# The first product of each expert in two halves of 512 columns, and the low terms of the second product last in each half

## The chip, the cores and the metric

The kernel runs on one core of a Trainium2 chip. A core has a matrix engine (TensorE, PE in the profile; its weight loads stand in a row of their own, PEld), VectorE (DVE), ScalarE (ACT), GpSimd (POOL) and SyncE (SP), which here issues most transfers. The engines run their own instructions in order and wait for each other by semaphores. The metric is the time of one execution in microseconds on the device.

## The reference

Attention with a window of 32 positions and 32 global tokens per batch gives 1088 rows of 512 numbers. A gate sends each row to the expert with the highest logit, up to 288 rows an expert, and a dense network of two products follows. The middle part is the one that matters here (sizes by the inputs: E = 8 experts, D = 512, F = 1024, capacity 288):

```python
logits = x @ w_gate
expert_idx = np.argmax(logits, axis=1)
...
disp[e, counts[e]] = x[i]          # if counts[e] < capacity
...
h = np.maximum(np.einsum('ecd,edf->ecf', disp, w1), 0.0)
y = np.einsum('ecf,efd->ecd', h, w2)
...
out[i] = gate_w[i] * y[expert_idx[i], pos[i]]
```

## The kernel before

The kernel is one program in three stages: attention with the gate, the experts, and the dense network. The order of instructions on each engine is the order in which the Python code writes them; no scheduler moves them, and the semaphores follow from the tiles that are read and written.

Products are made in float32r, each operand as a high part (rounded) and a low part (what the rounding left). A product is three terms: high times high, high times low, and low times high. So each weight chunk that lands (`raw`, 128x1024) is rounded to `H` by `weight_h` (L218 on ScalarE, L220 on VectorE for one chunk in eight) and the rest taken to `L` by `weight_l` (L230 on VectorE). Each expert has eight such chunks, four of w1 and four of w2, and its successor's chunks are converted while it runs. `split` (L598, L599) does the same for the rows: ScalarE rounds from PSUM, VectorE subtracts.

An expert's rows come in groups of 128, 128 and 32. The first group always runs (the first tile). The second and the third stand under branches on the expert's count (`rest`, the branch tiles). `expert_tile` makes one group. `mm1(q)` multiplies the rows with 256 columns of w1 in one PSUM buffer (8 matmuls with the high rows, 4 with the low rows) and takes the relu on ScalarE into `hs`. `tr(q)` turns `hs` by two transposes into a PSUM buffer of tag T, which has two, and splits that into `hh` and `hl`. `mm2(k)` multiplies the k-th 128 of them with 128 rows of w2: high with H, high with L, low with H, all eight into one PSUM buffer `py`. `bg()` is called eight times in a first tile and writes the background work: the weight conversions, the copy of the last expert's `py` to `ys` (L810), small steps for the gates, in experts 6 and 7 steps of the next stage's weights (L248 to L285), and in the third call the load of the expert's count into registers with a hint for the branch (L889 to L891). `mid(0)` turns the next expert's rows (`x_prep`, tiles `mx`, `x0h`, `x0l`). After expert 7 the rows of two token tiles are multiplied into the next stage's input, of which VectorE makes the low part at L1139.

Of the kernel before, what the change touches and what calls it, by code (L numbers as in the profile page):

```python
# [8 lines left out]
F32 = mybir.dt.float32  # L9
# [4 lines left out]
AF = mybir.ActivationFunctionType  # L14
# [4 lines left out]
P = 128  # L19
# [9 lines left out]
def tile_attention_moe_ffn(  # L29
# [23 lines left out]
    nc = tc.nc  # L53
# [10 lines left out]
    KD = DM // P  # L64
    KF = F // P
# [21 lines left out]
    def ps_tile(tag, name, hold=False):  # L87

        bank = psum[tag].pop(0)
        (held.setdefault(name, []) if hold else psum[tag]).append(bank)  # L90
        return pspool.tile([P, 512], F32, tag=bank, name=name, bufs=2 if bank == "T" else 1)
# [5 lines left out]
    def ps_a(name):  # L97
        return ps_tile("A", name)

    def ps_t(name):  # L100
        return ps_tile("T", name)
# [173 lines left out]
    def wide_h(g, c):  # L275
        if c == 0:
            unit_tiles(2 * E + g, 8)
        H, L = HL[2 * E + g]
        sl = slice(c * 512, (c + 1) * 512)
        nc.scalar.copy(H[:, sl], CV[g, c])  # L280

    def wide_l(g, c):
        H, L = HL[2 * E + g]
        sl = slice(c * 512, (c + 1) * 512)
        nc.vector.tensor_tensor(out=L[:, sl], in0=CV.pop((g, c)), in1=H[:, sl].bitcast(F32), op=ALU.subtract)  # L285
# [311 lines left out]
    def split(dst_h, dst_l, src):  # L597
        nc.scalar.copy(dst_h, src)  # L598
        nc.vector.tensor_tensor(out=dst_l, in0=src, in1=dst_h.bitcast(F32), op=ALU.subtract)  # L599
# [13 lines left out]
    for i in range(2):  # L613
        t = at.tile([P, 576], F32, name=f"pg{i}")
# [64 lines left out]
    for k in range(NS):  # L679
# [14 lines left out]
        if 5 <= k < 13:  # L694
            c = k - 5
# [38 lines left out]
    for ns, k0 in ((range(5), range(KD)),):  # L734
        for n in ns:
            x, at_ = parts[n]
# [24 lines left out]
    mo = mctx.enter_context(tc.tile_pool(name="mo", bufs=1))  # L761
# [50 lines left out]
    def base_store(e, eng):  # L812
        rows = groups[0][1]
        eng.dma_start(yd[1 + e * cap:1 + e * cap + rows, :], YB[e][:rows])
# [8 lines left out]
    def expert_tile(e, j, bg, mid):  # L823

        nm = f"{e}_{j}"
        rows = groups[j][1]
        w1h, w1l = W[2 * e]
        w2h, w2l = W[2 * e + 1]
        xh, xl = XH.pop((e, j))
        HS = {}  # L830
        hh = mo.tile([P, F], F32R, tag="hh", name=f"hh{nm}", bufs=1).rearrange("p (k t) -> p k t", k=KF)
        hl = mo.tile([P, F], F32R, tag="hl", name=f"hl{nm}", bufs=1).rearrange("p (k t) -> p k t", k=KF)
        py = ps_tile("V" if j and e < E - 1 else "Y", f"py{nm}")

        def mm1(q):
            ph = ps_a(f"ph{nm}{q}")
            fs = slice(256 * q, 256 * q + 256)
            for k in range(KD):
                nc.tensor.matmul(ph[:rows, :256], xh[:, k, :rows], w1h[:, k, fs], start=k == 0, stop=False)  # L839
                nc.tensor.matmul(ph[:rows, :256], xh[:, k, :rows], w1l[:, k, fs], start=False, stop=False)  # L840
            for k in range(KD):
                nc.tensor.matmul(ph[:rows, :256], xl[:, k, :rows], w1h[:, k, fs], start=False, stop=k == KD - 1)  # L842
            HS[q] = mo.tile([P, 256], F32, tag="hs", name=f"hs{nm}{q}", bufs=3)
            nc.scalar.activation(HS[q][:rows], ph[:rows, :256], AF.Relu)  # L844

        def tr(q):
            pt = ps_t(f"pt{nm}{q}")
            hs = HS.pop(q)
            for k in range(2):
                nc.tensor.transpose(pt[:, k * P:k * P + rows], hs[:rows, k * P:(k + 1) * P], ident[:rows, :rows])  # L850
            split(hh[:, 2 * q:2 * q + 2, :rows], hl[:, 2 * q:2 * q + 2, :rows],
                  pt[:, :256].rearrange("p (k t) -> p k t", k=2)[:, :, :rows])

        def mm2(k):
            a, c = hh[:, k, :rows], hl[:, k, :rows]
            nc.tensor.matmul(py[:rows], a, w2h[:, k, :], start=k == 0, stop=False)  # L856
            nc.tensor.matmul(py[:rows], a, w2l[:, k, :], start=False, stop=False)  # L857
            nc.tensor.matmul(py[:rows], c, w2h[:, k, :], start=False, stop=k == KF - 1)  # L858

        bg()  # L860
        mm1(0)
        mm1(1)
        bg()
        tr(0)
        mm1(2)
        bg()
        tr(1)
        mm1(3)
        bg()
        tr(2)  # L870
        mm2(0)
        mid(0)
        bg()
        mm2(1)
        tr(3)
        mm2(2)
        mid(1)
        bg()
        mm2(3)
        mm2(4)  # L880
        bg()
        mm2(5)
        mm2(6)
        bg()
        mm2(7)
        return py

    def count(e):
        vals[e] = nc.values_load(cnt[0:1, e:e + 1], engines=engs, min_val=0, max_val=cap)  # L889

        tc.mark_branch_hint_location(f"rest{e}_1", (vals[e] + (P - 1)) >> 8, engines=(ENG.PE, ENG.DVE, ENG.Activation))  # L891
# [96 lines left out]
    def job_h(u, c):  # L988
        weight_h(u, c, nc.vector if 4 * (u % 2) + c == 3 else nc.scalar)

    def job_l(u, c):
        weight_l(u, c, nc.vector)
        if wn[0] < len(wl) + 6:
            next_w()
# [8 lines left out]
    hl = [[lambda c=c: wide_h(0, c), lambda c=c: wide_l(0, c)] for c in range(4)]  # L1003
# [8 lines left out]
    for e in range(E):  # L1012
# [3 lines left out]
        def bg():  # L1016
            n = nbg[0]
            nbg[0] += 1
            if e > 0 and n == 2:
                count(e)  # L1020
            while late_l:
                job_l(*late_l.pop(0))
            for job in todo[:((2, 1, 1, 1, 1, 1, 1, 0) if e < E - 3 else (2, 2, 1, 1, 1, 1, 0, 0))[n]]:
                del todo[:1]
                job_h(*job)

                late_l.append(job)
            for f in wide[n] if wide else ():
                f()
            if e > 0 and small:  # L1030
                small.pop(0)()
            if n == (e < E - 1) and py_last is not None:
                base_out(*py_last)
                if e == E - 1:
                    base_store(e - 1, nc.sync)
            if n == 2 and py_last is not None and e < E - 1:
                base_store(e - 1, nc.sync)
            if e == 0 and n == 7:
                for i in range(E):
                    for r0, rows in groups[1:]:  # L1040
                        nc.sync.dma_start(yd[1 + i * cap + r0:1 + i * cap + r0 + rows, :], zero[:rows])
            if e == E - 1:
                for f in own.get(n, ()):
                    f()

        def mid(i):
            if i == 1 and e == 0:
                count(e)
            if i == 0 and e + 1 < E:
                x_prep(e + 1, 0)  # L1050
                if e + 2 < E:
                    x_load(e + 2, 0, 1)

        rest_load(e)
        py = expert_tile(e, 0, bg, mid)
# [78 lines left out]
    for h in range(2):  # L1134
        px = OWN["x"][h].rearrange("p (k n) -> p k n", k=2)
        xh, xl = (x.rearrange("p (a h) n -> p h a n", h=2)[:, h] for x in XC[0])
# [83 lines left out]
    ph = []  # L1220
# [189 lines left out]
```

## Time and profile before

| | us |
|---|---|
| median of 3 runs | 478.09 |
| lowest and highest | 477.2, 481.27 |
| the profiled execution | 479.32 |
| its span, first to last instruction | 477.5 |

| engine | busy us | share of the span |
|---|---|---|
| PE | 451.1 | 94% |
| PEld | 395.5 | 83% |
| DVE | 337.6 | 71% |
| ACT | 245.3 | 51% |
| POOL | 96.4 | 20% |

The rows further down come from one profiled execution. In a timeline a row is a start, a duration and an instruction or several alike; a matmul's duration includes its pipeline, so the distance between starts tells what one costs in a stream. In brackets stands how long the engine was idle before and what ended that; "issue" names nothing that the profile shows.

### The profile page before, as it was taken

What the parts mean: (1) busy time and instruction counts of PE and PEld (TensorE: products, weight loads), DVE (VectorE), ACT (ScalarE), POOL (GpSimd) and SP (SyncE); (2) the same over time, 40 slices, a digit from 0 to 9 for tenths busy, and PEclk for the clock granted to TensorE, in tenths of its full rate; (3) what the DMA queues carried; (4) which work ended last, traced back from release to release, by engine and by line L of the source; (5) the groups of instructions that cost most, each with busy time, mean ns of one, the idle gap of its engine ahead of it and who ended that gap; (6) DMA issues with size and microseconds to landing.
All of it is one profiled execution on the core that took longest, in us unless ns stands there. A gap on an engine that the chain in (4) does not pass through costs nothing. (4 is left out here: it accounts for less than half of the span.)

```text
span 477.5 us, 8782 instructions
## 1 busy us (share of the span) xinstructions
PE 451.1 (94%) x3163; PEld 395.5 (83%) x3164; DVE 337.6 (71%) x739; ACT 245.3 (51%) x556; POOL 96.4 (20%) x98
## 2 busy tenths in 40 slices
PE   8998899999999989899989799998999999999997
PEld 4776677788787878788878699998999999999997
DVE  4787498683166397754987875777788888979633
ACT  4768566273253466644776476455444344343311
POOL 1114355300000000000001271322213222232221
PEclk9999799999999998999999799999999999999999
DMA  8999544579348189982895531363222220000103
GB/s 267 289 329 364 184 143 134 184 271 366 138 145 286 56 275 298 333 286 75 275 347 176 168 113 56 113 231 113 75 89 89 88 89 1 1 0 1 66 1 121
DMA packets 34600, 79.24 MB, mean 166 GB/s; under 512 B 3761, under 2 KB 8497, under 8 KB 34546
## 3 DMA queue, kind: packets, MB, share of 16 engines
q1 hardware_dynamic: 31698, 70.40, 44.2%
q0 software_dynamic: 1408, 4.46, 2.9%
q10 hardware_dynamic: 1440, 3.67, 2.3%
q8 instruction: 33, 0.54, 0.5%
q14 instruction: 21, 0.17, 0.1%
HBM read 63.77 MB, written 14.75 MB: 164 GB/s over the span
## 5 line engine op out<-in xcount | busy, mean ns | idle before, releaser
L1157 PE MATMUL fh<-oldH,H 128*128 128x256 f32 (+1 forms) x256 | 66.8, 338 | 4.6 <-DVE oldH L1139 2.9
L230 DVE TENSOR_TENSOR L<-raw,H 128x1024 fp32r<-128x1024 f32 x56 | 66.8, 1218 | 1.8 <-issue 1.0
L218 ACT CAST H<-raw 128x1024 fp32r<-128x1024 f32 x57 | 59.3, 1061 | 15.2 <-PEq L896 13.0
L1197 PE MATMUL acc<-oldH,H 128*128 128x256 f32 (+2 forms) x240 | 65.0, 332 | 1.4 <-ACT H L280 1.0
L1157 PEld LDWEIGHTS fh<-oldH,H 128*128 128x128 f32 x256 | 46.9, 199 | 7.7 <-DVE oldH L1139 3.2
L1171 DVE SCALAR_TENSOR_TENSOR r<-r 128x256 f32<-128x256 f32 (+2 forms) x48 | 31.3, 652 | 23.6 <-ACT r L1162 23.5
L599 DVE TENSOR_TENSOR hl<-pt,hh 128x256 fp32r<-128x256 f32 (+1 forms) x48 | 19.3, 403 | 39.6 <-ACT hh L598 38.6
L1197 PE MATMUL acc<-oldH,L 128*128 128x256 f32 (+2 forms) x144 | 47.2, 328 | 0.0
L1197 PEld LDWEIGHTS acc<-oldH,H 128*128 128x128 f32 x240 | 43.3, 189 | 4.2 <-ACT H L280 1.5
L1183 ACT CAST oldH<-g 128x256 fp32r<-128x256 f32 (+2 forms) x36 | 17.9, 496 | 55.5 <-DVE g L1175 55.5
L844 ACT ACTIVATE hs<-ph 128x256 f32<-128x256 f32 (+1 forms) x48 | 18.6, 388 | 47.6 <-PE ph L842 46.6
L1157 PE MATMUL fh<-oldH,L 128*128 128x448 f32 (+1 forms) x128 | 42.5, 333 | 0.0
L1184 POOL TENSOR_TENSOR oldH<-g,oldH 128x256 fp32r<-128x256 f32 (+2 forms) x24 | 26.9, 1120 | 76.9 <-ACT oldH L1183 59.3
L856 PE MATMUL py<-H,hh 128*128 128x512 f32 (+1 forms) x96 | 40.6, 423 | 0.0
L1162 ACT ACTIVATE r<-fh,half 128x256 f32<-128x256 f32 (+2 forms) x48 | 27.1, 564 | 23.2 <-PE fh L1157 22.7
L839 PE MATMUL ph<-H,x0h 128*128 128x256 f32 x128 | 34.5, 301 | 4.0 <-PEq L896 2.1
L858 PE MATMUL py<-H,hl 128*128 128x512 f32 (+1 forms) x96 | 38.1, 397 | 0.0
L857 PE MATMUL py<-L,hh 128*128 128x512 f32 (+1 forms) x96 | 37.6, 392 | 0.0
L285 DVE TENSOR_TENSOR L<-co,H 128x512 fp32r<-128x512 f32 x32 | 23.2, 731 | 19.0 <-ACT H L280 19.0
L1157 PE MATMUL fh<-oldL,H 128*128 128x384 f32 x128 | 35.3, 340 | 0.4 <-DVE g L1175 0.4
L932 POOL DMA_INDIRECT yg_own<-yd,idx x2 | 2.3, 1138 | 156.7 <-ACT hs L844 156.4
L324 ACT ACTIVATE sm<-sm,ng 128x224 f32<-128x224 f32 x64 | 30.1, 477 | 4.6 <-DVE ng L313 4.5
(202 smaller groups left out, 1102.1 us busy)
## 6 DMA issues: line engine op xcount, KB each, us to landing
raw<-in_w_dram SPq DMA_DIRECT2D x64, 512.0 KB, 5.8
raw<-in_w_in_dram SPq DMA_DIRECT2D x14, 512.0 KB, 5.1
raw<-in_w_out_dram SPq DMA_DIRECT2D x12, 512.0 KB, 3.7
xd<-zero SPq DMA_DIRECT2D x16, 256.0 KB, 6.0
vt<-in_vx_dram SPq DMA_DIRECT2D x8, 320.0 KB, 5.0
xt<-xd SPq DMA_DIRECT2D x8, 256.0 KB, 5.0
yd<-zero SPq DMA_DIRECT2D x8, 256.0 KB, 4.6
yd<-ys SPq DMA_DIRECT2D x8, 256.0 KB, 4.8
```

Source lines behind the costliest of these rows:

```text
L218: nc.scalar.copy(dst, src)
L230: eng.tensor_tensor(out=L[:, sl], in0=RAW.pop((u, c)), in1=H[:, sl].bitcast(F32), op=ALU.subtract)
L324: nc.scalar.activation(SM[s][:, c, :], SM[s][:, c, :], AF.Exp, bias=NG[s][:, c:c + 1], scale=-1.0, accum_out=SUM[b][:, i, col:col + 1])
L839: nc.tensor.matmul(ph[:rows, :256], xh[:, k, :rows], w1h[:, k, fs], start=k == 0, stop=False)
L856: nc.tensor.matmul(py[:rows], a, w2h[:, k, :], start=k == 0, stop=False)
L857: nc.tensor.matmul(py[:rows], a, w2l[:, k, :], start=False, stop=False)
L858: nc.tensor.matmul(py[:rows], c, w2h[:, k, :], start=False, stop=k == KF - 1)
L1157: nc.tensor.matmul(ph[:, :n], w[:, k, :], XC[c][i // 2][:, k, :], start=n_ == 0, stop=n_ == len(terms) - 1)
L1162: nc.scalar.activation(RS[f % 2][:, :n], ph[:, :n], AF.Relu, bias=half, scale=0.5)
L1171: nc.vector.scalar_tensor_tensor(out=r[:, :n], in0=r[:, :n], scalar=1.0, in1=r[:, :n], op0=ALU.min, op1=ALU.mult)
L1184: nc.gpsimd.tensor_tensor(out=gl[:, :n], in0=gt[:, :n], in1=gh[:, :n].bitcast(F32), op=ALU.subtract)
L1197: nc.tensor.matmul(a[:, :n], p[:, ds], q, start=f == 0 and i == 0, stop=f == nfl - 1 and i == 2)
```

## The change

The first product is made in two halves of 512 columns instead of four quarters of 256, with 24 matmuls instead of 48. A half can be written in parts: the second half's first four matmuls stand ahead of the first half's transposes. The relu and both steps of the split work on 512 columns, twice a tile instead of four times. `hs` has one buffer of 512 columns instead of three of 256. In the second product each half of four k takes its eight matmuls with high rows first and its four with low rows last. The calls of `bg` and `mid` stand at other places of the tile, in the same number.

```diff
--- before.py
+++ after.py
@@ -827,62 +827,61 @@
         w1h, w1l = W[2 * e]
         w2h, w2l = W[2 * e + 1]
         xh, xl = XH.pop((e, j))
-        HS = {}
+        HS, HP = {}, {}
         hh = mo.tile([P, F], F32R, tag="hh", name=f"hh{nm}", bufs=1).rearrange("p (k t) -> p k t", k=KF)
         hl = mo.tile([P, F], F32R, tag="hl", name=f"hl{nm}", bufs=1).rearrange("p (k t) -> p k t", k=KF)
         py = ps_tile("V" if j and e < E - 1 else "Y", f"py{nm}")
 
-        def mm1(q):
-            ph = ps_a(f"ph{nm}{q}")
-            fs = slice(256 * q, 256 * q + 256)
-            for k in range(KD):
-                nc.tensor.matmul(ph[:rows, :256], xh[:, k, :rows], w1h[:, k, fs], start=k == 0, stop=False)
-                nc.tensor.matmul(ph[:rows, :256], xh[:, k, :rows], w1l[:, k, fs], start=False, stop=False)
-            for k in range(KD):
-                nc.tensor.matmul(ph[:rows, :256], xl[:, k, :rows], w1h[:, k, fs], start=False, stop=k == KD - 1)
-            HS[q] = mo.tile([P, 256], F32, tag="hs", name=f"hs{nm}{q}", bufs=3)
-            nc.scalar.activation(HS[q][:rows], ph[:rows, :256], AF.Relu)
+        def mm1(q, lo, hi):
+            if lo == 0:
+                HP[q] = ps_a(f"ph{nm}{q}")
+            fs = slice(512 * q, 512 * q + 512)
+            terms = [(xh, w, k) for k in range(KD) for w in (w1h, w1l)] + [(xl, w1h, k) for k in range(KD)]
+            for i in range(lo, hi):
+                x, w, k = terms[i]
+                nc.tensor.matmul(HP[q][:rows], x[:, k, :rows], w[:, k, fs], start=i == 0, stop=i == len(terms) - 1)
+            if hi == len(terms):
+                HS[q] = mo.tile([P, 512], F32, tag="hs", name=f"hs{nm}{q}", bufs=1)
+                nc.scalar.activation(HS[q][:rows], HP.pop(q)[:rows], AF.Relu)
 
         def tr(q):
             pt = ps_t(f"pt{nm}{q}")
             hs = HS.pop(q)
-            for k in range(2):
+            for k in range(4):
                 nc.tensor.transpose(pt[:, k * P:k * P + rows], hs[:rows, k * P:(k + 1) * P], ident[:rows, :rows])
-            split(hh[:, 2 * q:2 * q + 2, :rows], hl[:, 2 * q:2 * q + 2, :rows],
-                  pt[:, :256].rearrange("p (k t) -> p k t", k=2)[:, :, :rows])
-
-        def mm2(k):
-            a, c = hh[:, k, :rows], hl[:, k, :rows]
-            nc.tensor.matmul(py[:rows], a, w2h[:, k, :], start=k == 0, stop=False)
-            nc.tensor.matmul(py[:rows], a, w2l[:, k, :], start=False, stop=False)
-            nc.tensor.matmul(py[:rows], c, w2h[:, k, :], start=False, stop=k == KF - 1)
+            split(hh[:, 4 * q:4 * q + 4, :rows], hl[:, 4 * q:4 * q + 4, :rows],
+                  pt.rearrange("p (k t) -> p k t", k=4)[:, :, :rows])
+
+        def mm2(q, lo, hi):
+
+            terms = [(hh, w, k) for k in range(4) for w in (w2h, w2l)] + [(hl, w2h, k) for k in range(4)]
+            for i in range(lo, hi):
+                h, w, k = terms[i]
+                nc.tensor.matmul(py[:rows], h[:, 4 * q + k, :rows], w[:, 4 * q + k, :],
+                                 start=q == i == 0, stop=q == 1 and i == len(terms) - 1)
 
         bg()
-        mm1(0)
-        mm1(1)
+        mm1(0, 0, 12)
         bg()
+        mm1(1, 0, 4)
         tr(0)
-        mm1(2)
         bg()
+        mm1(1, 4, 12)
+        bg()
+        mm2(0, 0, 6)
         tr(1)
-        mm1(3)
-        bg()
-        tr(2)
-        mm2(0)
+        mm2(0, 6, 9)
         mid(0)
         bg()
-        mm2(1)
-        tr(3)
-        mm2(2)
+        mm2(0, 9, 12)
+        mm2(1, 0, 1)
         mid(1)
         bg()
-        mm2(3)
-        mm2(4)
+        mm2(1, 1, 6)
         bg()
-        mm2(5)
-        mm2(6)
+        mm2(1, 6, 10)
         bg()
-        mm2(7)
+        mm2(1, 10, 12)
         return py
 
     def count(e):
```

ScalarE, first tile of expert 2, as it stands before (`raw` casts are the background work, `ys` the last product's copy):

```order
L218 CAST H_2379<-raw_1_1970 128x1024
L820 UNCONDITIONAL_BRANCH
L844 ACTIVATE hs_00_2397<-ph_00_2384 128x256
L844 ACTIVATE hs_01_2412<-ph_01_2399 128x256
L218 CAST H_2379<-raw_2_2025 128x1024
L810 COPY ys_2422<-py_0_1930 128x512
L598 CAST hh_0_2376<-pt_00_2424 128x256
L844 ACTIVATE hs_02_2442<-ph_02_2429 128x256
L889 TENSOR_LOAD cnt
L891 ISA
L1406 BRANCH_PREFETCH_HINT
L598 CAST hh_0_2376<-pt_01_2478 128x256
```

and as it stands with the change:

```order
L218 CAST H_2163<-raw_1_1847 128x1024
L820 UNCONDITIONAL_BRANCH
L845 ACTIVATE hs_00_2181<-ph_00_2168 128x512
L218 CAST H_2163<-raw_2_1894 128x1024
L810 COPY ys_2191<-py_0_1822 128x512
L598 CAST hh_0_2160<-pt_00_2198 128x512
L888 TENSOR_LOAD cnt
L890 ISA
L1405 BRANCH_PREFETCH_HINT
L845 ACTIVATE hs_01_2247<-ph_01_2193 128x512
L218 CAST H_2252<-raw_0_1942 128x1024
L598 CAST hh_0_2160<-pt_01_2262 128x512
```

The second relu stands behind the first copy to `hh` and the count's load instead of ahead of the third cast, and two entries of 512 columns stand for four of 256.

TensorE, the same tile, around its first transposes, before:

```order
L840 MATMUL ph_01_2399<-L_1932,x0h 128x256
L842 MATMUL ph_01_2399<-H_1931,x0l 128x256 x4
L850 MATMUL pt_00_2424<-ident,hs_00_2397 128x128 x2
L839 MATMUL ph_02_2429<-H_1931,x0h 128x256
L840 MATMUL ph_02_2429<-L_1932,x0h 128x256
L839 MATMUL ph_02_2429<-H_1931,x0h 128x256
```

and with the change:

```order
L842 MATMUL ph_00_2168<-H_1823,x0l 128x512 x4
L842 MATMUL ph_01_2193<-H_1823,x0h 128x512
L842 MATMUL ph_01_2193<-L_1824,x0h 128x512
L842 MATMUL ph_01_2193<-H_1823,x0h 128x512
L842 MATMUL ph_01_2193<-L_1824,x0h 128x512
L851 MATMUL pt_00_2198<-ident,hs_00_2181 128x128 x4
L888 TENSOR_LOAD cnt
L890 ISA
L1405 BRANCH_PREFETCH_HINT
L842 MATMUL ph_01_2193<-H_1823,x0h 128x512
L842 MATMUL ph_01_2193<-L_1824,x0h 128x512
```

The transposes of `hs` have four matmuls between them and the last one of their own half, where they had twelve, and the count's load follows them.

TensorE, the same tile, where the second product begins, before:

```order
L850 MATMUL pt_02_2505<-ident,hs_02_2442 128x128 x2
L856 MATMUL py_0_2378<-H_2053,hh_0_2376 128x512
L857 MATMUL py_0_2378<-L_2054,hh_0_2376 128x512
L858 MATMUL py_0_2378<-H_2053,hl_0_2377 128x512
L798 MATMUL mx_0_0_2513<-ident,xt_0_2072 128x128 x4
L856 MATMUL py_0_2378<-H_2053,hh_0_2376 128x512
L857 MATMUL py_0_2378<-L_2054,hh_0_2376 128x512
L858 MATMUL py_0_2378<-H_2053,hl_0_2377 128x512
L850 MATMUL pt_03_2530<-ident,hs_03_2496 128x128 x2
```

and with the change:

```order
L860 MATMUL py_0_2162<-L_1913,hh_0_2160 128x512
L851 MATMUL pt_01_2262<-ident,hs_01_2247 128x128 x4
L860 MATMUL py_0_2162<-H_1912,hh_0_2160 128x512
L860 MATMUL py_0_2162<-L_1913,hh_0_2160 128x512
L860 MATMUL py_0_2162<-H_1912,hl_0_2161 128x512
L798 MATMUL mx_0_0_2272<-ident,xt_0_1939 128x128 x4
L860 MATMUL py_0_2162<-H_1912,hl_0_2161 128x512 x3
L860 MATMUL py_0_2162<-H_1912,hh_0_2160 128x512
```

The matmuls with `hl` stand ninth to twelfth of a half instead of each third, and the second transposes behind six matmuls with `hh`.

## Rows read from the trace of the kernel before

**Rows 1.** The page's part 1: busy time, share of the span and instructions.

```profile
PE 451.1 (94%) x3163; PEld 395.5 (83%) x3164; DVE 337.6 (71%) x739; ACT 245.3 (51%) x556; POOL 96.4 (20%) x98
```

**Rows 2.** Windows, first tiles of experts 3, 4, 6: length, busy us, clock, DMA.

```profile
175.10:191.60 16.50, 14.32 (x84) 12.85 (x85) 13.35 (x22) 10.44 (x19) 0.00 (x0) 0.90 0.92 301
191.60:206.70 15.10, 13.51 (x88) 11.73 (x88) 12.22 (x21) 10.47 (x19) 0.00 (x0) 1.00 0.97 328
234.60:249.20 14.60, 13.04 (x85) 11.20 (x85) 12.98 (x16) 11.73 (x20) 0.00 (x0) 1.00 0.99 357
```

**Rows 3.** Groups by line: busy us, mean ns | idle before, releasers.

```profile
L599 DVE TENSOR_TENSOR hl<-pt,hh 128x256 fp32r<-128x256 f32 (+1 forms) x48 | 19.3, 403 | 39.6 <-ACT hh L598 38.6 <-ACTq L896 1.0
...
L844 ACT ACTIVATE hs<-ph 128x256 f32<-128x256 f32 (+1 forms) x48 | 18.6, 388 | 47.6 <-PE ph L842 46.6 <-DVE L L230 0.6
...
L599 DVE TENSOR_TENSOR x0l<-mx,x0h 128x512 fp32r<-128x512 f32 x7 | 4.8, 683 | 0.1
...
L810 ACT COPY ys<-py 128x512 f32<-128x512 f32 (+1 forms) x9 | 4.7, 540 | 1.4 <-PE py L858 1.4
...
L598 ACT CAST x0h<-mx 128x512 fp32r<-128x512 f32 x7 | 4.3, 612 | 0.0
```

**Rows 4.** Timeline of VectorE, experts 6 and 7: start, us, what, [idle before].

```profile
239.92 0.42 DVE L599 TENSOR_TENSOR hl<-pt,hh 128x256 fp32r<-128x256 f32 x1 [1.23 <-ACT hh L598]
...
269.84 1.29 DVE L1139 TENSOR_TENSOR oldH<-po,oldH 128x512 fp32r<-128x512 f32 x2 [2.01 <-DVEq L896]
```

**Rows 5.** Waits of PE: total us, times, longest.

```profile
PE fh L1157 <- DVE oldH L1139: 2.9, 1, 2.9
...
PE ph L842 <- DVE xl L599: 1.4, 2, 0.8
...
PE pt L850 <- DVE hl L599: 0.6, 2, 0.3
```

**Rows 6.** Timeline of PE, expert 0, first tile.

```profile
98.10 0.28 PE L839 MATMUL ph<-H,x0h 128*128 128x256 f32 x1
...
98.69 0.28 PE L840 MATMUL ph<-L,x0h 128*128 128x256 f32 x1
...
103.88 0.39 PE L856 MATMUL py<-H,hh 128*128 128x512 f32 x1
...
106.61 0.39 PE L856 MATMUL py<-H,hh 128*128 128x512 f32 x1
```

**Rows 7.** Timeline of ACT, expert 2.

```profile
161.62 2.00 ACT L218 CAST H<-raw 128x1024 fp32r<-128x1024 f32 x2 [3.85 <-PEq L896]
...
165.10 0.38 ACT L844 ACTIVATE hs<-ph 128x256 f32<-128x256 f32 x1 [1.03 <-PE ph L842]
165.39 1.04 ACT L218 CAST H<-raw 128x1024 fp32r<-128x1024 f32 x1
...
166.80 0.39 ACT L598 CAST hh<-pt 128x256 fp32r<-128x256 f32 x1
```

**Rows 8.** Timeline of PE, expert 1, branch tile.

```profile
148.31 0.28 PE L840 MATMUL ph<-L,xh 128*128 128x256 f32 x1
149.39 0.50 PE L842 MATMUL ph<-H,xl 128*128 128x256 f32 x2 [0.80 <-DVE xl L599]
```

**Rows 9.** Timeline of PE, experts 3 and 4, the stops.

```profile
177.45 0.28 PE L842 MATMUL ph<-H,x0l 128*128 128x256 f32 x1
179.76 0.52 PE L842 MATMUL ph<-H,x0l 128*128 128x256 f32 x3 [2.03 <-issue]
...
193.45 0.28 PE L840 MATMUL ph<-L,x0h 128*128 128x256 f32 x1
195.12 0.39 PE L839 MATMUL ph<-H,x0h 128*128 128x256 f32 x1 [1.39 <-issue]
```

**Rows 10.** The page's part 3, instruction transfers.

```profile
q8 instruction: 33, 0.54, 0.5%
```

**Rows 11.** Windows, expert 3 after the first stop.

```profile
180.80:184.20 3.40, 3.40 (x19) 3.40 (x18) 1.43 (x2) 2.54 (x6) 0.00 (x0) 0.50 0.90 316
```

## The prediction

> **What bounds the kernel now.** I read the page's busy line first [rows 1]: TensorE's matmuls fill 94% of the span and no other engine comes near, so the question is which stretch of TensorE's row the change shortens. The windows cut at the starts of the first tiles of experts 3, 4 and 6 [rows 2] show the stage it edits: such a tile takes 14.6 to 16.5 us, TensorE is idle in it for 1.6 to 2.2 us, and VectorE is busy for 12.2 to 13.4 us of it, so VectorE is second and close. DMA is at 0.92 to 0.99 of its time there. The relu row has 48 entries, four to a tile [rows 3]: twelve tiles run, eight first ones and four that a branch takes. Ten of them belong to experts 0 to 5.
>
> Experts 6 and 7 I treat apart. VectorE's row there [rows 4] runs nearly without a gap from the first low part of expert 6 (239.92) until it waits 2.01 us at the end of the last branch and makes the low part of the next stage's input at 269.84; TensorE waits 2.9 us for that [rows 5]. So a faster TensorE in experts 6 and 7 is worth nothing, unless VectorE's first low part comes earlier, and that one follows from the start of expert 6. What the ten earlier tiles save, expert 6 starts earlier by, and the rest of the program follows.
>
> **The change part by part.**
>
> *Wider matmuls.* Of 256 columns TensorE starts one each 0.118 us (98.10 to 98.69, five), of 512 one each 0.2275 us (103.88 to 106.61, twelve) [rows 6]. A tile's first product is 48 of the first kind, 5.66 us, and becomes 24 of the second, 5.46 us: 0.20 us a tile, **2.0 us** over ten. The weight loads (some 0.19 us each) lie beside matmuls at both widths and are worth nothing by themselves. The eight transposes of a tile stay eight.
>
> The Trainium skill (TensorE: Matmul & The Clock Gate, Back-to-back issue gap) gives a spacing of columns divided by 2.4 GHz plus 2.5 ns, 109 and 216 ns. By that the ten tiles would give 0.6 us, as an estimate from that page; the rows have more for each matmul, and they decide.
>
> *Transposes behind a longer relu.* Before, the first transposes of a tile stand a whole block of twelve matmuls behind their own relu, 1.4 us. Now four matmuls of the next half stand between. A matmul of 512 columns ends 0.39 us after its start [rows 6]; a relu of 512 columns I put at 0.60 us, between the copies of 512 columns at 0.54 and 0.61 [rows 3]; with some 0.25 us for hand-overs and for the transposes' own weight load, the transposes can stream 1.24 us after the last matmul of the half started. Their turn comes after five spacings, 1.14 us. The wait is 0.1 us a tile. In tiles of experts 1 to 7 the register load for the branch now stands right behind those transposes, which may show by as much. I take 0.13 us a tile, **1.3 us lost** over ten; bounds 0 (the relu at twice half of its present price less its start) and 0.4 (a hand-over more, and the load in full).
>
> *ScalarE's file.* In a first tile ScalarE runs relu, a weight cast (1.04 us), the copy of the last product (0.54 us) and only then the copy of the high parts (expert 2: second relu 165.10, cast 165.39, high parts 166.80) [rows 7]. The order stays, with one relu for two. Successive entries there overlap by some 0.1 us, so from the last matmul's start: relu 0.49, cast 0.99, copy 1.94, high parts 2.44 to 3.04. The second product's first matmul wants them at 1.24, some 0.5 for four transposes and 8 x 0.2275, together 3.56. Half a microsecond is left, so I cost it at nothing; the cover is those eight matmuls, and without it each tile would pay up to the cast's 1.05 us. The second half has more room. VectorE itself does a little less: two low parts of 0.68 us for four of 0.40 [rows 3].
>
> *Low parts of the input.* In a branch tile the first product's low terms wait for VectorE's low part: TensorE stands from its matmul at 148.31 to 149.39 [rows 8], and 1.4 us in two tiles in all [rows 5]. These terms are the ninth and later. Eight matmuls last 0.88 us longer at 512 columns, so the wait falls to 0.1 to 0.3 us, for **1.2 us** won.
>
> *Low parts of the rows last.* The second product's low terms move from third place to ninth, behind all high terms of their half. Waits of transposes for VectorE's low part, 0.6 us in two places [rows 5], go with it, since a half has its own transpose buffer; one lies in expert 5 and counts, **0.3 us**. VectorE's last entry of a tile stands where it stood: in expert 6 the first low part comes some 0.2 us later and lasts 0.27 us longer, and two entries fewer give that back.
>
> *Waits for code.* TensorE stops twice in the middle of a first product with nothing to wait for: 2.03 and 1.39 us, put down to "issue", after 177.45 and 193.45 [rows 9], that is after some 21 and 16 matmuls of experts 3 and 4, and each of these tiles follows a branch that was not taken. The page has a queue of instruction transfers, 33 of them for 0.54 MB, 16 KB each [rows 10], for the 6,327 matmuls and loads that ran [rows 1] and what is jumped over. An expert has 524 of TensorE's instructions in the program's listing, loads counted, so 42 instructions into expert 3 and 32 into expert 4 are nearly one place in steps of 256, which a transfer may hold. So I read the stops as the end of a block of code reached too soon after a jump. The change takes 24 matmuls and their loads out of each of an expert's three tile bodies: 380 instructions for 524. By the same counting the block ends then lie 232, 111 and 123 instructions into experts 3, 4 and 6, over 10 us behind the jump, and both stops go: **3.4 us**. After the first of them TensorE's granted clock is 0.50, its lower level of 1.2 GHz, for 3.4 us [rows 11]; with no stop of that length ahead of it this half goes too, **1.7 us**. But one block end falls at the very start of expert 7, and one jump into expert 3 reaches a block asked for only 2 us before. I take **1.5 us lost** there; bounds 0 and 3.4, what the two stops cost now.
>
> The Trainium skill (Runtime: NRT & Kernel Launch, Instruction fetch mechanics) has blocks of 256 instructions fetched in sequence, and says that a taken branch to a place outside the current two blocks waits for a fetch. The stops agree in kind, though here they come after the jump has gone well. The same section gives TensorE room for 2048 instructions; if so, a whole expert would fit and these stops would have another cause, which is the second rival.
>
> The sum: 2.0 - 1.3 + 1.2 + 0.3 + 3.4 + 1.7 - 1.5 = 5.8 us less. The profiled execution took 479.32 us (span 477.5 and 1.8 around it), 1.2 us above the median of the runs shown; 478.09 - 5.8 = **472.3 us**.
>
> **The rivals.**
>
> *The stops stay.* Whatever makes them, the changed program has as many. For it: I infer the block ends, nothing names them. Then 2.0 - 1.3 + 1.2 + 0.3 = 2.2 us are left: 475.9 us.
>
> *The transfers bind.* Experts 3 and 4 move 301 and 328 GB/s for 16.5 and 15.1 us, 9.9 MB, and the fastest tile moves 357 [rows 2]: 27.8 us at that rate against 31.6 now and 25.8 by my sum. Then 2 us of the gain are lost: 474.3 us. Against: these are the tiles in which the queue is never empty, but a branch tile with no loads of its own follows expert 4, and what is late there has time.
>
> *ScalarE is late in every first tile, and it is slower.* The mechanism is the file above: if ScalarE reaches the relu over half a microsecond late, the high parts come after the eight matmuls that cover them, and the second product waits for a cast, 1.05 us. With the transposes waiting for another in each of eight first tiles that is 8 x 1.05 = 8.4 us, less the 2.2 us of the second case: 484.3 us. For it: one buffer for the relu's rows, and all slack in the tile is now 0.5 us where it was 3. Against: ScalarE is idle for 1.03 us before its second relu, and the two casts ahead of the first end at 163.62 [rows 7], 1.7 us into a tile whose first half now lasts 2.7.
>
> **How the numbers follow.** No change and 1% (4.8 us) can't be told apart well by a measurement of this kernel, so that is the bound. The forecast has 0.42, with 468.5 to 474.5 (the new waits at 0 or 3.4, the wait for transposes at 0 or 0.4, the 2.0 us at the end of the branch, which is of the same kind, gone or not). The stops stay: 0.27. Transfers: 0.10. Slower: 0.12. What is left, 0.09, I spread over both ends. Faster by over 1% is under 473.3: most of the first case, a third of the third, some of the rest, 0.46. Slower by over 1%: 0.13. The range of 467.5 to 479 leaves out the slower case and a little at each end.
>
> **What would show it.** First products of 24 matmuls at 0.2275 us; a gap of about 0.1 us ahead of the first transposes in each tile and none ahead of the second product; no wait for the low part over 0.3 us; no "issue" stop inside experts 3 and 4 and a granted clock of 1.00 through the experts; VectorE still last at the end of expert 7. The prediction is wrong if TensorE waits for ScalarE's high parts by several tenths in each first tile, or if stops of 1 to 2 us turn up at other jumps.

## The result and the profile after

The changed kernel took 465.19 us (median of 4 runs, 464.59 to 466.67) against 477.64 us before (475.97 to 481.27): a ratio of 0.9736 [0.9693, 0.978], 12.5 us less where 5.8 were forecast. The profiled executions are 479.32 us before and 465.16 us after, 14.2 us apart. Ratios here, with their 95% intervals in brackets, are taken over undisturbed runs, so they are not always the quotient of the medians. An experiment's ratio is to the kernel before as it ran beside that experiment.

The page of the changed kernel, its busy line, the granted clock in 40 slices and the queue of instruction transfers, answers to [rows 1, 10]:

```profile
PE 445.2 (96%) x2875; PEld 375.6 (81%) x2876; DVE 335.9 (72%) x715; ACT 242.6 (52%) x508; POOL 95.5 (21%) x98
...
PEclk9999999999999999999999899999999999999999
...
q8 instruction: 29, 0.48, 0.4%
```

TensorE's work fell by 5.9 us only (451.1 to 445.2), less than half of what the kernel gained. So most of the gain is idle time that went, and the next step is to ask in which stretch. The windows of the first tiles of experts 3, 4 and 6 [rows 2]:

```profile
170.90:183.90 13.00, 12.86 (x60) 10.05 (x61) 12.32 (x20) 10.21 (x14) 0.00 (x0) 1.00 0.99 337
183.90:197.50 13.60, 13.33 (x64) 10.55 (x64) 12.93 (x21) 10.44 (x15) 0.00 (x0) 1.00 1.03 384
224.20:237.40 13.20, 12.88 (x61) 10.05 (x61) 11.82 (x14) 11.16 (x15) 0.00 (x0) 1.00 0.99 353
```

They last 13.0, 13.6 and 13.2 us for 16.5, 15.1 and 14.6, TensorE is idle 0.1 to 0.3 us in each for 1.6 to 2.2, and the clock is at 1.00. In the first two 9.6 MB land in 26.6 us, at 337 and 384 GB/s. TensorE's timeline in these tiles answers to [rows 6, 8, 9]; each expert's first matmul gives the tile lengths:

```profile
92.39 0.47 PE L842 MATMUL ph<-H,x0h 128*128 128x512 f32 x1
...
145.82 0.39 PE L842 MATMUL ph<-L,xh 128*128 128x512 f32 x1
146.49 1.20 PE L842 MATMUL ph<-H,xl 128*128 128x512 f32 x4 [0.28 <-DVE xl L599]
...
170.91 0.47 PE L842 MATMUL ph<-H,x0h 128*128 128x512 f32 x1
...
174.43 0.40 PE L842 MATMUL ph<-L,x0h 128*128 128x512 f32 x1
174.66 0.65 PE L851 MATMUL pt<-ident,hs 128*128 128x128 f32 x4
175.26 0.49 PE L842 MATMUL ph<-H,x0h 128*128 128x512 f32 x1
...
224.18 0.47 PE L842 MATMUL ph<-H,x0h 128*128 128x512 f32 x1
...
237.36 0.50 PE L842 MATMUL ph<-H,x0h 128*128 128x512 f32 x1 [0.32 <-ACTq L895]
```

Between 170.91 and 174.43 sixteen matmuls start one after the other, the second 0.31 us behind the first and each later one 0.23 behind the last, with no stop; the transposes come 0.23 us behind the matmul ahead of them, so no wait shows; the matmul behind them comes 0.60 us after their start. For the tile lengths three starts of the kernel before are needed that were not shown:

```profile
94.54 0.35 PE L839 MATMUL ph<-H,x0h 128*128 128x256 f32 x1
...
234.64 0.36 PE L839 MATMUL ph<-H,x0h 128*128 128x256 f32 x1
...
249.19 0.35 PE L839 MATMUL ph<-H,x0h 128*128 128x256 f32 x1 [1.20 <-PEq L896]
```

VectorE's timeline at the end of the experts [rows 4], ScalarE's in expert 2 [rows 7] and TensorE's waits [rows 5], all of the changed kernel:

```profile
256.91 1.29 DVE L1138 TENSOR_TENSOR oldH<-po,oldH 128x512 fp32r<-128x512 f32 x2 [0.21 <-ACT ca L248]
```

```profile
160.98 0.60 ACT L845 ACTIVATE hs<-ph 128x512 f32<-128x512 f32 x1 [1.44 <-PE ph L842]
161.48 1.04 ACT L218 CAST H<-raw 128x1024 fp32r<-128x1024 f32 x1
162.41 0.59 ACT L810 COPY ys<-py 128x512 f32<-128x512 f32 x1
162.89 0.60 ACT L598 CAST hh<-pt 128x512 fp32r<-128x512 f32 x1
```

```profile
PE fh L1156 <- DVE oldH L1138: 1.7, 1, 1.7
...
PE ph L842 <- DVE xl L599: 0.3, 1, 0.3
```

Cut at these starts (and at 175.11, the start of expert 3 before), the two spans divide as follows.

| stretch | before us | after us | difference |
|---|---|---|---|
| attention, to the experts' first matmul | 94.54 | 92.39 | -2.15 |
| experts 0 to 2, six tiles | 80.57 | 78.52 | -2.05 |
| experts 3 to 5, four tiles | 59.53 | 53.27 | -6.26 |
| expert 6 | 14.55 | 13.18 | -1.37 |
| expert 7, to VectorE's low part | 20.65 | 19.55 | -1.10 |
| the rest, dense stage | 207.7 | 206.5 | -1.2 |

Attention is the same code in both. Over the profiles of this study its length goes from 91.24 us (fifth experiment, granted clock 1.00 throughout) to 96.62 us (eleventh, 10.2 us at 0.50). Four profiles of kernels that do the old work have 93.3 us on average, ten of kernels that do the new work 93.2, so I put those 2.15 us down to the execution. What the edit itself can have moved stands in the four stretches behind it; the dense stage comes up again below.

### The profile page after: what moved, and what is told of

It is laid out like the page before. It is cut to its first block, busy times and chain, and to the rows that moved or that the text cites. A ratio compares the mean times of both kernels' runs of the same rounds, so it can differ in the third digit from the quotient of the medians.

```text
span 463.4 us, 8110 instructions
## 1 busy us (share of the span) xinstructions
PE 445.2 (96%) x2875; PEld 375.6 (81%) x2876; DVE 335.9 (72%) x715; ACT 242.6 (52%) x508; POOL 95.5 (21%) x98
## 5 line engine op out<-in xcount | busy, mean ns | idle before, releaser
L218 ACT CAST H<-raw 128x1024 fp32r<-128x1024 f32 x57 | 58.0, 1049 | 10.3 <-PEq L895 8.4
L599 DVE TENSOR_TENSOR hl<-pt,hh 128x512 fp32r<-128x512 f32 (+1 forms) x24 | 15.7, 654 | 35.6 <-ACT hh L598 35.6
L860 PE MATMUL py<-H,hh 128*128 128x512 f32 (+1 forms) x96 | 38.7, 403 | 0.0
L845 ACT ACTIVATE hs<-ph 128x512 f32<-128x512 f32 (+1 forms) x24 | 14.4, 598 | 41.2 <-PE ph L842 41.2
L270 DVE SCALAR_TENSOR_TENSOR co<-raw,ca 128x512 uint32<-128x512 uint32 x32 | 31.6, 995 | 0.9
L860 PE MATMUL py<-H,hl 128*128 128x512 f32 (+1 forms) x96 | 28.5, 401 | 0.0
```

What stands on the lines that cost most here:

```text
L218: nc.scalar.copy(dst, src)
L270: nc.vector.scalar_tensor_tensor(out=o, in0=lo, scalar=29, in1=a, op0=ALU.logical_shift_right, op1=ALU.bitwise_or)
L860: nc.tensor.matmul(py[:rows], h[:, 4 * q + k, :rows], w[:, 4 * q + k, :], start=q == i == 0, stop=q == 1 and i == len(terms) - 1)
```

## The experiments

Theory 1: much of the gain is waits for code, which hang on where in a program a jump lands. Its rival: the edit's own matmuls and order.

**Programs that differ in dead instructions alone.** The first and the eighth take the changed kernel, the second the kernel before; all add this in the branch of a third row group that isn't taken:

```diff
+            if j == 2 and e in {1: 106, 3: 68}:        # second: {1: 90}; eighth: {1: 112, 3: 68}
...
+                idle = ps_a(f"idle{e}")
...
+                for _ in range({1: 106, 3: 68}[e]):
+                    nc.tensor.matmul(idle, zero.bitcast(BF16)[:, :P], zero.bitcast(BF16)[:, :512], start=True, stop=True)
```

> The changed kernel with matmuls that never run: 106 in the branch of expert 1's third row group and 68 in that of expert 3's, two instructions each, jumped over for these counts. What runs is the changed kernel's work in its order; only the places in TensorE's program move, so that by steps of 256 instructions a block ends some 20 instructions into experts 3 and 4, where the kernel before had its stops (2.03 and 1.39 us). Theory 1 (the stops are waits for code and hang on place alone): both stops come back, 1.4 to 2.7 us each, with or without a half granted clock behind the first (1.7 us): 3 to 7 us above 465.2, so 468 to 472. Rival (the wider and fewer matmuls removed the stops, or the stops were the run's): no stop, 465.2 within 0.7.

467.52 us, 0.978 [0.9731, 0.9829]. TensorE's timeline:

```profile
185.92 0.40 PE L842 MATMUL ph<-H,x0l 128*128 128x512 f32 x1
186.93 0.97 PE L842 MATMUL ph<-H,x0l 128*128 128x512 f32 x3 [0.61 <-issue]
...
229.48 0.60 PE L851 MATMUL pt<-ident,hs 128*128 128x128 f32 x4 [0.58 <-issue]
```

In expert 4 a stop is back, behind the ninth matmul, where the counting put it. In expert 3 there is none, and an unplanned one stands in expert 6, with an instruction transfer 2.2 to 2.5 us ahead of it (DMA view of 227.0 to 227.3 us). Half the effect that I expected, 2.3 us over the changed kernel's median; the two intervals overlap, so here too the trace says more than the time.

> The kernel before with 90 matmuls that never run (180 instructions) in the branch of expert 1's third row group. Its quarters, relus and order stay; the ends of blocks of 256 instructions move from 32 to 42 to some 110 to 120 instructions into experts 3 and 4, far behind the jump. Theory 1: the stops of 2.03 and 1.39 us go, and the half granted clock behind the first with them: 3.4 to 5.4 us below the kernel before, 472 to 474 against 477.6, less about 1 if another place is hit instead. Rival (the stops belong to the 48 narrow matmuls and their loads): 477.6 within 1.

475.51 us against 477.73, 0.9972 [0.9938, 1.0006]: by time alone this doesn't tell the theory from the rival. The trace does: experts 3 and 4 have no "issue" stop. Expert 3 starts at 172.92 and its low terms run on (row below); its profiled execution took 473.24 us. VectorE's wait at the end stays:

```profile
172.92 0.35 PE L839 MATMUL ph<-H,x0h 128*128 128x256 f32 x1 [0.40 <-PEq L896]
173.94 0.63 PE L842 MATMUL ph<-H,x0l 128*128 128x256 f32 x4
```

```profile
263.39 1.29 DVE L1145 TENSOR_TENSOR oldH<-po,oldH 128x512 fp32r<-128x512 f32 x2 [1.80 <-DVEq L896]
```

> The first experiment with six more matmuls that never run in expert 1's branch (112 for 106), so that a block's end by my counting falls some 8 instructions into experts 3 and 4 instead of 20; the work that runs stays the changed kernel's. In the first experiment TensorE went on 2.4 us after an instruction transfer showed, as in the kernel before. Theory (the wait is the time from the jump to the landing, less the work in front of the block's end): with 12 instructions, 1.4 us of matmuls, less in front, expert 3's wait appears and expert 4's grows from 0.78 to some 2 us: 2 to 5 us above the changed kernel and 1 to 3 above the first experiment, so 468 to 471. Rival (place inside the tile does not matter): as the first experiment, 467.5 within 0.7.

468.46 us, 0.9803 [0.9735, 0.9871], 3.3 us over the changed kernel's median. The size is as expected, though its interval too overlaps the changed kernel's; the place is not: the wait stands ahead of expert 3's first matmul, put down to TensorE's sequencer, and expert 4 has none over 0.3 us. The second fence is the DMA view of 170.5 to 170.7 us:

```profile
169.00 1.07 PE L860 MATMUL py<-H,hl 128*128 128x512 f32 x4
173.11 0.47 PE L842 MATMUL ph<-H,x0h 128*128 128x512 f32 x1 [3.04 <-PEq L895]
```

```profile
q8 instruction: 1, 0.02, 31.6%
```

Six dead matmuls more than in the first experiment turn a start with no wait in the view into one of 3.04 us at that jump, in one profiled execution of each. The work that runs is the same, so place makes the wait, and my counting is off by some instructions.

**VectorE's program.** The same with memsets of a scratch tile that never run, 39 in the changed kernel (fifth), 89 in the second experiment's kernel (sixth):

```diff
+            if j == 2 and e == 1:
...
+                for _ in range(39):                     # sixth: 89
+                    nc.vector.memset(idle_v, 0.0)
```

> The changed kernel with 39 VectorE instructions that never run, in the branch of expert 1's third row group. They put VectorE's program behind expert 1 back by as much as the change had shortened it there; its work and order stay the changed kernel's. Theory (VectorE's 2.01 us at the end of expert 7's branch was a wait for code that hangs on place): it comes back, TensorE's wait for the low part of the dense stage's input grows from 1.7 to about 3 us, 466.5 to 467.3 against 465.2. Rival (it went because VectorE comes to that branch with less work queued): 465.2 within 0.5 and a gap of 0.2 us as in the changed kernel.

465.23 us, 0.9729 [0.9662, 0.9796], with the gap as in the changed kernel: the theory missed here, and the rival came.

```profile
256.06 1.29 DVE L1142 TENSOR_TENSOR oldH<-po,oldH 128x512 fp32r<-128x512 f32 x2 [0.22 <-ACT ca L248]
```

> The kernel before with the 90 matmuls of the second experiment that never run, and with 89 VectorE instructions that never run in the same branch, which put VectorE's program where it stands in the changed kernel by steps of 128. What is left against the changed kernel is then the edit's own work. Theory: no stop in experts 3 and 4 as in the second experiment, and VectorE's 1.80 us before the dense stage shrinks to some 0.2: 1.3 to 1.9 us under the second experiment's 475.5, so 473.6 to 474.2; a span of 469.5 to 470.2 in the profile against 471.4. Rival (VectorE's wait hangs on the order of its work): 475.5 within 0.7.

472.75 us against 478.49, 0.9867 [0.9808, 0.9927], some 1 us under the expected time. The profiled span, 471.8 us, misses the 469.5 to 470.2 expected: attention takes 94.3 us in it for 91.8 in the second experiment's. VectorE's wait is gone, with the old kernel's work and order:

```profile
264.70 1.29 DVE L1149 TENSOR_TENSOR oldH<-po,oldH 128x512 fp32r<-128x512 f32 x2 [0.21 <-ACT ca L248]
```

TensorE's wait for it is 1.7 us where the second experiment has 3.3. So place alone can take the 2.01 us of [rows 4] away. It doesn't bring them back: the fifth gave VectorE's program back the 39 instructions that the change takes from it, with the changed work, and got no wait. That the wait is one for code is borne out by the DMA view of the kernel before, 267.6 to 267.8 us. VectorE runs out of work at 267.83; just before, an instruction transfer of 8 KB stands in a queue of its own, and VectorE goes on 2.0 to 2.2 us behind it.

```profile
q14 instruction: 1, 0.01, 17.2%
```

In the second experiment such a transfer stands 1.8 to 2.0 us ahead of the end of its wait (261.4 to 261.6); in the changed kernel the last one (254.5 to 254.7) comes while VectorE still has 2 us of work.

**The order alone, and the width alone.** The third keeps the halves and takes the low term third in each k; the fourth keeps the quarters and takes the low terms last:

```diff
-            terms = [(hh, w, k) for k in range(4) for w in (w2h, w2l)] + [(hl, w2h, k) for k in range(4)]
+            terms = [(h, w, k) for k in range(4) for h, w in ((hh, w2h), (hh, w2l), (hl, w2h))]
```

```diff
+        terms2 = []
+        for s in (0, 4):
+            terms2 += [(hh, w, s + k) for k in range(4) for w in (w2h, w2l)] + [(hl, w2h, s + k) for k in range(4)]
```

> The changed kernel, but the second product takes its low term third in each k, as before the change; width, places of transposes and number of instructions are the changed kernel's. It tells the part of the low terms' order. Forecast's term: 0.3 us in all, so 465.2 to 465.8. Rival (the order carries the part of the gain that the forecast missed, since the second product's third matmul now waits for VectorE's low part, about 0.68 us and a hand-over behind the high part in each of twelve tiles): 4 to 8 us above, 469 to 473.

465.07 us, 0.9712 [0.9666, 0.9758]: with the halves the order is worth nothing that can be measured, and its rival falls.

> The kernel before with its quarters of 256 columns, but in the second product the eight high terms of each half of four k ahead of its four low terms; number and place of all instructions as before. Forecast's term: 0.3 us, so 477.0 to 477.6, with both stops in experts 3 and 4 still there (theory 1: order of equal counts does not move a block). Rival (the order carries the missed gain): 471 to 474.

481.11 us, 1.0033 [0.999, 1.0077]: not told apart from the kernel before, though over the 477.0 to 477.6 expected. Both stops are there, as the theory has it, and a third has grown: ahead of expert 7, where the kernel before waits 1.20 us, this one waits 4.02. The second fence is the DMA view of 247.2 to 247.4 us.

```profile
177.88 0.52 PE L842 MATMUL ph<-H,x0l 128*128 128x256 f32 x3 [2.22 <-issue]
...
192.47 0.39 PE L839 MATMUL ph<-H,x0h 128*128 128x256 f32 x1 [1.95 <-issue]
...
249.86 0.55 PE L839 MATMUL ph<-H,x0h 128*128 128x256 f32 x1 [4.02 <-PEq L899]
```

```profile
q8 instruction: 1, 0.02, 29.0%
```

The number of instructions is the old kernel's, and the wait at the same place costs 1.2 us in one profiled execution and 4.0 in the other. Whether the order of the terms or the execution makes that difference isn't shown.

**The count's load.** The seventh moves one call of the background work:

```diff
         tr(0)
+        mm1(1, 4, 8)
         bg()
-        mm1(1, 4, 12)
+        mm1(1, 8, 12)
```

> The changed kernel with its third call of the background work, which holds the load of the expert's count into registers, behind four more matmuls of the second half instead of right behind the first transposes. The profile after shows TensorE's first matmul behind these transposes some 0.2 us late in the seven first tiles that load a count, and the transposes themselves on time. Theory (the load is paid in full only where it stands behind transposes that have just waited, since nothing is queued to cover it): 7 x 0.2 = 1.4 us below 465.2, so 463.8. Rival (a register load costs TensorE 0.2 us wherever it stands): 465.2 within 0.4.

464.5 us, 0.971 [0.9658, 0.9761]. The matmul behind the transposes now comes 0.41 us after their start instead of 0.60:

```profile
174.53 0.39 PE L842 MATMUL ph<-L,x0h 128*128 128x512 f32 x1
174.75 0.66 PE L851 MATMUL pt<-ident,hs 128*128 128x128 f32 x4
175.16 0.48 PE L842 MATMUL ph<-H,x0h 128*128 128x512 f32 x1
```

From the experts' first matmul to expert 7's it is 143.62 us (92.84 to 236.46) for 144.97: 1.35 us in the six tiles there that load a count, 0.2 us each. But from expert 6's start to VectorE's low part both take 32.7 us (223.50 to 256.22; 224.18 to 256.91): what TensorE saves in experts 6 and 7 is lost again, and the rest is too little for the runs to tell it from no change.

**VectorE's file ahead of the dense stage.** The ninth moves four steps of the next weights behind the low part, the tenth does so in the seventh's kernel, the eleventh moves two there; the twelfth is the changed kernel again:

```diff
-                ab[4:6] + hl[2] + hl[3], ws[2]],
+                ab[4:6] + hl[2] + hl[3], ws[2][:4]],
...
         nc.vector.tensor_tensor(out=xl, in0=px, in1=xh.bitcast(F32), op=ALU.subtract)
+    for f in ws[2][4:]:
+        f()
```

> The changed kernel with the last four VectorE steps of the next stage's weight words (two of L265, two of L270, 2.58 us) written behind the low part of the dense stage's input instead of ahead of it. In the changed kernel this low part starts at 256.91, though the high part that it reads is ready some 1.5 us sooner, and TensorE waits 1.7 us for it. Theory (experts 6 and 7 end by VectorE's file, not by TensorE or by a transfer): TensorE's wait falls to some 0.4 us, 1.0 to 1.5 us below the changed kernel of this call. Rival (the words are wanted at once by the dense stage's first weights, so the wait moves there): within 0.5 of it.

> The last experiment's words behind the low part together with the count's load behind four more matmuls. If both terms are of the size read (0.2 us in each of six tiles up to expert 6, then the wait at the end of VectorE's file): 2.2 to 2.7 us below the changed kernel of this call, so some 462.7. Rival (the two cover each other, since both end in VectorE's file of experts 6 and 7): only 1.2 to 1.5 below.

> As the last, but with two of the four word steps moved (L270, 1.29 us) instead of four. Theory: VectorE comes to the low part 1.2 us sooner, which is nearly all that the high part allows (1.5), and the dense stage gets half as much work back: within 0.4 of the last. Rival (the dense stage has room for all of it): 0.3 to 0.5 above the last.

> The changed kernel again, unchanged, as the one that the three others of this call are held against: 465.2 within 0.5. Its second profile tells which stops belong to the program and which to the one execution: by the theory no stop over 0.6 us in experts 3 and 4 and a gap of 0.2 us at VectorE's low part, with the half-clock stretches of attention and of the dense stage free to differ.

465.99, 465.03, 464.48 and 465.0 us; 0.975 [0.9724, 0.9776], 0.9729 [0.9702, 0.9755], 0.9724 [0.9695, 0.9752] and 0.9739 [0.9713, 0.9765]. Held against the twelfth, the three lie 1.0 us above it, level with it, and 0.5 us below it, with intervals that overlap. No theory's gain came, and by their numbers the rivals did not either: the ninth's and the tenth's are missed by 0.5 us and more, and the eleventh came out under the tenth instead of above. The ninth's rival is right in kind: TensorE's wait for the low part goes, and another of the same size stands 7 us later, for VectorE's `g` rows of the dense stage:

```profile
PE fh L1158 <- DVE g L1176: 1.6, 1, 1.6
```

No version here beats the changed kernel by what can be measured. The twelfth repeats its tiles (13.0 and 13.7 us for experts 3 and 4) with no stop.

## Why the prediction was wrong

The direction was right, and so was the reading of the two stops in experts 3 and 4; the gain was twice the forecast. The steps in the prediction's order:

- *Wider matmuls, 2.0 us:* right. The first product's spacings added up over the eleven tiles ahead of expert 7, without its waits and the starts behind transposes, are 2.2 us shorter than in the second experiment's kernel, 0.20 us a tile. (The formula of 109 and 216 ns that the prediction set aside is given in the Trainium skill, TensorE: Matmul & The Clock Gate, Back-to-back issue gap, for a matmul by itself and not for a stream; the sum didn't use it.)
- *Transposes behind a longer relu, 1.3 us lost:* about the right size, by luck. They never waited for the relu: in every tile of 128 rows they start 0.23 us behind the matmul ahead of them. The 0.25 us for hand-overs and the weight load have no row of before; in expert 2 the relu ends at 161.58 and the transposes start at 161.64. What came instead is the register load named beside it, 0.2 us in seven tiles, five of them among the ten of the sum; the seventh experiment gets 1.35 us back in the six ahead of expert 7.
- *ScalarE's file, nothing:* right. High parts end at 163.49 in expert 2 and no wait for them shows in any tile.
- *Low parts of the input, 1.2 us:* right; 1.4 us of waits became 0.3.
- *Low parts of the rows last, 0.3 us:* too small. With the halves the order gives nothing (third experiment); the waits of transposes for VectorE, 0.6 us in two places, stay with the order alone (fourth) and went with the halves. More lies in the spacings inside the second product, which the sum left out: over ten tiles they come to 1.4 us less than before and 1.7 less than in the second and sixth experiments, by the starts in TensorE's timelines. A matmul that follows the first one behind transposes comes 0.31 us after it for 0.23 elsewhere; a tile had three such places and has two. And late matmuls with `hl` are gone, as in expert 1 before, where spacings of 0.37 and 0.34 us stand:

```profile
145.11 0.39 PE L857 MATMUL py<-L,hh 128*128 128x512 f32 x1
145.48 0.50 PE L858 MATMUL py<-H,hl 128*128 128x512 f32 x1
145.82 0.40 PE L856 MATMUL py<-H,hh 128*128 128x512 f32 x1
```

`hl` takes 15.7 us on VectorE for 19.3:

```profile
L599 DVE TENSOR_TENSOR hl<-pt,hh 128x512 fp32r<-128x512 f32 (+1 forms) x24 | 15.7, 654 | 35.6 <-ACT hh L598 35.6
```

These five came to 2.2 us in ten tiles by the forecast. Measured, the six tiles of experts 0 to 2, which have no stop in either kernel, are 2.05 us shorter. Against the sixth experiment, whose tiles run from 94.30 to 245.09,

```profile
94.30 0.36 PE L839 MATMUL ph<-H,x0h 128*128 128x256 f32 x1
...
245.09 0.36 PE L839 MATMUL ph<-H,x0h 128*128 128x256 f32 x1 [0.88 <-PEq L896]
```

eleven tiles gain 5.8 us (150.79 to 144.97), of which 1.5 are longer waits at its experts' starts, so 4.3 of the edit's own. For the ten tiles of the sum that is 3.4 us, and 3.6 against the second experiment. So the sum was 1.2 to 1.4 us low, about what the second product's spacings hold.

- *Stops in experts 3 and 4, 3.4 us:* right, both are gone, in the second and sixth experiments by dead instructions alone.
- *Half clock behind the first, 1.7 us:* it went; its price was nearer 1.4. Without the stops (second and sixth experiments) the old kernel's two tiles are 4.8 us shorter, waits at their starts left out, and 3.42 of that are the stops. The dense stage is 205.4 us where its clock is never at half (seventh experiment, 256.22 to 461.6), 206.5 with 3.4 us of it and 207.7 with twice that, 1.1 us each. (The sixth and second experiments, also with 3.4 us, have 207.1 and 208.1, but 0.5 and 1.4 us more of TensorE's waits there.)
- *New code waits, 1.5 us lost:* **this is the step that failed.** I counted a block's end at the start of expert 7 and charged it. There was no new wait in either profile of the changed kernel, and two old ones of the same kind went: expert 7's start waits 0.32 us for 1.20, and VectorE's 2.01 us ahead of the low part are 0.21. The prediction let the second widen its range and put it at nothing in the sum, and doesn't name the first. Together with the charge that is 4.2 us of the 6.7 that were missed; the five terms above, too low together, are another 1.2 to 1.4.
- *Experts 6 and 7 worth nothing:* right of a faster TensorE (32.7 us in the seventh experiment, whatever TensorE saves), wrong as a statement on the stretch: it became 2.5 us shorter, about what those two waits held.

Of the rivals none came. Transfers reached 384 GB/s, over the 357 at which I had capped them.

What stays open: between the sixth experiment's 472.75 us and the changed kernel's 465.2 some 7.5 us lie, in the two profiles 8.5. Of these 5.8 stand in experts 0 to 6 and 1.9 in attention, the same code with 3.4 us at half clock in both; the cause of the 1.9 wasn't found. What brings VectorE's wait back wasn't found either. That place alone removes waits of TensorE (second experiment) and VectorE (sixth) and makes one of TensorE (eighth) is shown, in one profiled execution each. That blocks of 256 do it is inferred from places, of which the first experiment's expert 4 and the second fit, and the eighth only within a few instructions.

The Trainium skill (Runtime: NRT & Kernel Launch, Instruction fetch mechanics) says that a taken branch to a place outside the current two blocks waits for a fetch. The eighth experiment's 3.04 us ahead of the first matmul behind a jump agrees in kind. The stops of [rows 9] come some 16 to 21 matmuls after the jump, so they neither bear it out nor speak against it.

## What to carry to other kernels

In a program with branches, count the waits for code (idle time put down to "issue" or to an engine's own sequencer) as a term of every edit that changes the number of instructions: here those that went (3.4, 0.9 and 1.8 us, and a half clock behind one) are more than the 4.3 us that the edit saved in eleven tiles, and they can go either way. Before an edit is praised or dropped, make the same kernel once with dead instructions in a branch that isn't taken; if that moves the time, the edit has not been measured yet. A wait of one engine that is removed close to a stage bound by another (words moved behind the low part, the count's load in experts 6 and 7) came back here a few us later.

## What was not expected of the hardware

- TensorE went on 2.4 to 2.6 us after an instruction transfer showed, in most of the stops looked at: transfers within 177.1 to 177.4 and 192.6 to 192.8 us before (next matmuls at 179.76 and 195.12), 247.2 to 247.4 in the fourth experiment (249.86), 170.5 to 170.7 in the eighth (173.11). Ahead of expert 7 in the kernel before it was 3.0 us (transfer within 246.1 to 246.4, next matmul at 249.19). What differs is how long after a tile's first matmul the transfer shows: 2.0 to 2.3 us in expert 3 before (first matmul at 175.11), 0.4 to 0.7 in expert 4 of the first experiment (184.00; transfer within 184.4 to 184.7, next matmul at 186.93).
- A half granted clock (0.50, 1.2 GHz) of 3.4 us cost 1.1 us in the dense stage and some 1.4 in expert 3 before, not half of 3.4, and stretches of it came and went between executions of kernels with the same code there: none, 3.4, 6.8 or 10.2 us in attention. Not every stop had one behind it: none followed the 3.04 us in the eighth experiment and the 2.22 in the fourth, one followed the fourth's 1.95 us and one began within its 4.02.
- A register load cost TensorE 0.2 us right behind the first transposes of a tile (next matmul 0.60 us after their start), and nothing that shows with four plain matmuls in between (0.41 us).
